# Score buffers, PV batches and lent banks in a fused attention and FFN block on one Trainium2 core

## The chip, the cores and the metric

The kernel runs on one core of a Trainium2 chip. The metric is the device time of one execution in microseconds (us). The median of the runs is quoted, and the profiles are of single executions, whose span is some 2 us shorter than the time of the same run.

## The reference, cut to what matters

One adaptive-layernorm transformer block: sequence S = 2048, width D = 1024, 32 query heads of 32 channels that share one key and one value head, FFN width 3584, bfloat16 data.

```python
h = layernorm(x) * (1 + ca) + sa            # sa, ca, ga, sb, cb, gb = silu(c) @ w_mod
q = h @ wq                                  # 32 heads of 32 channels
k, v = h @ wk, h @ wv                       # one head
p = softmax(q @ k.T * 32 ** -0.5)
x = x + ga * ((p @ v) @ wo)
h = layernorm(x) * (1 + cb) + sb
x = x + gb * ((silu(h @ w1) * (h @ w3)) @ w2)
```

## The kernel before

The kernel lists its operations as a graph, orders them on each engine with a list scheduler that uses guessed durations, and then emits a fixed order per engine. The program does not change this order at run time; a wrong guess in it is paid as a wait.

The queries are worked off in four blocks of 512. A block's attention has 8 head groups (4 heads each) of 16 key tiles. One **step** is one key tile for 4 heads: four score matmuls that run side by side in the array (four take 0.61 us together in the first timeline below), exponentials of 4 x 512 columns on ScalarE, and PV, which multiplies the exponentials with V. After a block's attention come its output projection, a layernorm and the FFN (called the post work). The post work of block b runs on TensorE in between the steps of block b+1. Hence nothing can fill TensorE in block 0, and the last block's post work stands alone at the end.

The kernel divides PSUM, the memory that TensorE writes its results to, into eight banks of 512 float32 columns. Before the change, five hold scores, one accumulates PV over 16 key tiles, and two (PB) serve everything else:

```python
S5 = nc.alloc_psum_tensor("S5", [P, 5, 512], F32)
A = nc.alloc_psum_tensor("A", [P, 512], F32)
PB = [nc.alloc_psum_tensor("PB%d" % i, [P, 512], F32) for i in range(2)]
# ... in attention, step i; u = i % 6 is the exponential buffer
s1 = 3 + i % 2
# four matmuls into banks 0, 1, 2 and s1                      writes "S3" and ("S1", s1)
e.activation(U[:, u, 0:3, :], S5[:, 0:3, :], ACT.Exp, scale=SCALE)    # 1536 columns, reads "S3"
e.activation(U[:, u, 3, :], S5[:, s1, :], ACT.Exp, scale=SCALE)       # 512 columns, reads ("S1", s1)
# ... after every second step: PV of two key tiles into A; VectorE sums U for the denominators
```

The three-bank part "S3" exists once. The scores of step i+1 can start only when the 1536-column exponential of step i has ended, and until they arrive ScalarE has just the 512-column exponential of step i to do. Call the ScalarE work that is left in that time the **cover**.

The softmax here doesn't subtract the row's maximum and nothing guards it: scores larger than these inputs give would overflow.

## Time and profile before

| | before |
|---|---|
| median of 4 runs (range) | 1398.92 us (1396.92 to 1401.57) |
| span of the profiled run | 1396.4 us |
| step 16 / 128 / 511 of 512 starts | 92.0 / 337.4 / 1196.7 us |
| last exponential ends | 1198.7 us |
| left after it (post work of block 3) | 197.7 us |

The first lines of the page give the busy time of each engine, then the busy share in tenths in 40 slices of the span, and the clock granted to TensorE in tenths of full speed. PE is TensorE, ACT is ScalarE, DVE is VectorE.

```profile
PE 1209.6 (87%) x8689; PEld 424.9 (30%) x8689; DVE 939.8 (67%) x1174; ACT 1046.8 (75%) x1142; POOL 17.3 (1%) x34
...
PE   4498985555899999988899999978999999789997
...
ACT  2378998888889999888899998989999989311100
...
PEclk9597995555899999998999999979999999889999
```

From about the third slice to the 34th, ScalarE is nearly always busy; the last six slices have almost no ScalarE work. TensorE is half idle, at half clock, in slices 7 to 10, which are the rest of block 0.

Groups of instructions; after the bar stand busy time and mean duration in ns, after the second bar the idle time just before them and what ended it. L613 and L615 are the two exponentials, L606 the scores.

```profile
L613 ACT ACTIVATE UREG<-S 128x1536 bf16<-128x1536 f32 x512 | 744.1, 1453 | 150.7 <-PE S L606 140.1
...
L606 PE MATMUL S<-QT,KT 32*128 32x512 bf16 x2048 | 222.5, 425 | 121.5 <-ACT UREG L613 118.3
L615 ACT ACTIVATE UREG<-S 128x512 bf16<-128x512 f32 x512 | 305.7, 597 | 0.0
```

ScalarE waits 140.1 us for scores, always before the large exponential, never before the small one. The timeline shows how, in a stretch of block 0 where TensorE has nothing else to do (start and duration in us, engine, line, operation):

```profile
286.01 1.45 ACT L613 ACTIVATE UREG<-S 128x1536 bf16<-128x1536 f32 x1 [0.23 <-PE S L606]
287.36 0.59 ACT L615 ACTIVATE UREG<-S 128x512 bf16<-128x512 f32 x1
287.51 0.11 PEld L606 LDWEIGHTS S<-QT,KT 32*128 32x128 bf16 x4 [2.06 <-ACT UREG L613]
287.52 0.61 PE L606 MATMUL S<-QT,KT 32*128 32x512 bf16 x4 [1.56 <-ACT UREG L613]
...
288.18 1.45 ACT L613 ACTIVATE UREG<-S 128x1536 bf16<-128x1536 f32 x1 [0.23 <-PE S L606]
```

The large exponential ends at 286.01 + 1.45 = 287.46, its successor starts at 288.18: a **round trip** of 0.72 us through TensorE. The small exponential covers all but 0.23 us of it. A step takes 288.18 - 286.01 = 2.17 us. Nearly all steps between 205 and 330 us are like this one; three of them, at the ends of head groups, take 3.64 us, as 16 matmuls for the denominators (1.90 us) stand before the scores, so that the mean there is 2.25 us. Without the wait a step would take 1.83 us: consecutive starts are 1.35 us apart after a large exponential, and about 0.48 us after a small one.

With post work in the mix, TensorE is full as well, and the scores also stand behind FFN matmuls (L711) that the fixed order put first:

```profile
460.58 1.68 PE L711 MATMUL PB<-QT,WREG 128*128 128x512 bf16 x7
...
461.63 0.63 ACT L615 ACTIVATE UREG<-S 128x512 bf16<-128x512 f32 x1
462.20 0.10 PEld L606 LDWEIGHTS S<-QT,KT 32*128 32x128 bf16 x4 [0.42 <-ACT UREG L613]
...
462.65 1.45 ACT L613 ACTIVATE UREG<-S 128x1536 bf16<-128x1536 f32 x1 [0.39 <-PE S L606]
```

Busy time by stretch: length, then busy us (and instructions) of each engine, granted clock, DMA share, GB/s. The first stretch is block 0 with query projections to do, the second the rest of block 0, the third block 1 with post work, the last the post work of block 3.

```profile
91.50:205.00 113.50, 104.78 (x929) 37.21 (x928) 91.20 (x108) 103.16 (x107) 0.00 (x0) 0.91 0.21 66
205.00:330.00 125.00, 65.94 (x496) 11.22 (x492) 68.70 (x66) 107.92 (x111) 0.00 (x0) 0.51 0.12 28
400.00:600.00 200.00, 198.16 (x1428) 67.85 (x1427) 148.16 (x172) 182.78 (x205) 0.00 (x0) 1.00 0.38 97
1200.00:1300.00 100.00, 88.18 (x409) 39.57 (x410) 46.72 (x75) 10.76 (x18) 1.47 (x3) 0.89 0.31 90
```

At the end, each of the eight groups of W2 (28 matmuls, L722) waits for the eviction of the previous one and its transpose (L732), so groups follow each other every 7.28 us although 28 matmuls need 6.06, at 0.216 us from start to start:

```profile
1339.91 6.21 PE L722 MATMUL PB<-HREG,WREG 128*128 128x512 bf16 x28
1346.96 0.40 PE L732 MATMUL PB<-IDENT,HREG 128*128 128x128 bf16 x4 [0.85 <-DVE HREG L725]
1347.19 6.21 PE L722 MATMUL PB<-HREG,WREG 128*128 128x512 bf16 x28
```

### The profile page before, as it was taken

To read this page: it belongs to the slowest core of one execution; us is meant where nothing else is said; L and a number is where in the kernel's file an instruction comes from. 1 tells how busy PE (TensorE), PEld (TensorE's weight loads), DVE (VectorE), ACT (ScalarE), POOL (GpSimd) and SP (SyncE) were. 2 spreads that over 40 slices of the span, in tenths; PEclk is the share of its full clock that TensorE was granted. 3 is DMA by queue.
4 is the path that set the end of the run, shared out by engine and by line. 5 is a ranking of instruction groups with operands and counts; after the bars stand their busy time and mean duration, and the time that the engine had idled before them with its cause. 6 is when DMAs were issued, how large, how long until landed. Compare 5 with 4: busy or idle time off the path is not lost.

```text
span 1396.4 us, 21161 instructions
## 1 busy us (share of the span) xinstructions
PE 1209.6 (87%) x8689; PEld 424.9 (30%) x8689; DVE 939.8 (67%) x1174; ACT 1046.8 (75%) x1142; POOL 17.3 (1%) x34
## 2 busy tenths in 40 slices
PE   4498985555899999988899999978999999789997
PEld 3233320000233333322333333322333333234443
DVE  5777775555777777668877876678777766644421
ACT  2378998888889999888899998989999989311100
POOL 1000000000000000000000000000000000000000
PEclk9597995555899999998999999979999999889999
DMA  8306013000024334450133334421333345225544
GB/s 319 122 31 197 1 34 80 1 1 0 1 61 120 93 97 102 85 116 25 46 106 91 107 102 80 87 80 31 91 106 107 91 88 98 57 63 154 146 79 110
DMA packets 252928, 118.93 MB, mean 85 GB/s; under 512 B 120736, under 2 KB 244640, under 8 KB 252832
## 3 DMA queue, kind: packets, MB, share of 16 engines
q1 hardware_dynamic: 252832, 117.59, 31.6%
q8 instruction: 68, 1.11, 0.3%
q14 instruction: 28, 0.23, 0.1%
HBM read 113.38 MB, written 4.19 MB: 84 GB/s over the span
## 4 chain that ended last, share of the span: by engine, by line
PE 77%; ACT 11%; DVE 7%; issue 3%; POOL 1%; DMA 0%; SPq 0%; DVEq 0%; POOLq 0%; ACTq 0%
PE PB L703 15%; PE PB L711 15%; PE PB L722 14%; PE S L606 13%; ACT UREG L613 9%; PE A L624 7%; PE PB L682 4%; PE PB L506 4%; PE PB L658 3%; DVE ST L421 2%; DVE UREG L646 2%; ACT UREG L615 1%; DVE XN L438 1%; PE PB L452 1%; PE PB L490 1%
## 5 line engine op out<-in xcount | busy, mean ns | idle before, releaser
L613 ACT ACTIVATE UREG<-S 128x1536 bf16<-128x1536 f32 x512 | 744.1, 1453 | 150.7 <-PE S L606 140.1
L646 DVE TENSOR_TENSOR UREG<-UREG 128x2048 bf16<-128x2048 bf16 x256 | 310.9, 1214 | 82.8 <-ACT UREG L615 82.4
L606 PE MATMUL S<-QT,KT 32*128 32x512 bf16 x2048 | 222.5, 425 | 121.5 <-ACT UREG L613 118.3
L615 ACT ACTIVATE UREG<-S 128x512 bf16<-128x512 f32 x512 | 305.7, 597 | 0.0
L703 PE MATMUL PB<-QT,WREG 128*128 128x512 bf16 x896 | 226.6, 386 | 1.3 <-DVE QT L467 1.3
L640 DVE TENSOR_TENSOR UREG<-UREG 128x2048 bf16<-128x2048 bf16 x128 | 155.6, 1215 | 106.3 <-ACT UREG L615 105.7
L711 PE MATMUL PB<-QT,WREG 128*128 128x512 bf16 x896 | 222.6, 381 | 0.0
L722 PE MATMUL PB<-HREG,WREG 128*128 128x512 bf16 x896 | 214.3, 380 | 0.0
L624 PE MATMUL A<-UREG,V 128*32 128x512 bf16 x2048 | 178.3, 429 | 6.5 <-ACT UREG L615 5.6
L606 PEld LDWEIGHTS S<-QT,KT 32*128 32x128 bf16 x2048 | 52.2, 92 | 350.9 <-ACT UREG L613 320.7
L706 ACT ACTIVATE HREG<-PB 128x512 bf16<-128x512 f32 x112 | 67.0, 599 | 116.3 <-PE PB L703 116.3
L708 DVE SCALAR_TENSOR_TENSOR HREG<-HREG,PB 128x512 bf16<-128x512 bf16 x112 | 76.0, 679 | 88.9 <-ACT HREG L706 88.9
L667 DVE RECIPROCAL DSB<-DSB 128x128 f32<-128x128 f32 x128 | 116.7, 932 | 0.9
L703 PEld LDWEIGHTS PB<-QT,WREG 128*128 128x128 bf16 x896 | 80.1, 98 | 118.8 <-issue 43.0
L711 PEld LDWEIGHTS PB<-QT,WREG 128*128 128x128 bf16 x896 | 81.0, 98 | 111.9 <-issue 29.0
L722 PEld LDWEIGHTS PB<-HREG,WREG 128*128 128x128 bf16 x896 | 79.2, 98 | 108.0 <-issue 30.3
L714 DVE TENSOR_TENSOR HREG<-HREG,PB 128x512 bf16<-128x512 bf16 x112 | 76.7, 685 | 20.3 <-PE PB L711 18.8
L682 PE MATMUL PB<-WO,QT 128*128 128x512 bf16 x256 | 67.9, 414 | 4.9 <-DVE QT L669 4.9
L506 PE MATMUL PB<-HREG,WREG 128*128 128x512 bf16 x256 | 63.9, 385 | 0.1
L725 DVE TENSOR_SCALAR HREG<-PB,MODC 128x512 bf16<-128x512 f32 x32 | 24.0, 749 | 53.6 <-PE PB L722 53.6
L624 PEld LDWEIGHTS A<-UREG,V 128*32 128x32 bf16 x2048 | 31.8, 96 | 85.1 <-issue 38.6
L452 PE MATMUL PB<-IDENT,XN 128*128 128x128 bf16 x256 | 28.1, 263 | 26.8 <-DVE XN L438 17.5
(56 smaller groups left out, 436.1 us busy)
## 6 DMA issues: line engine op xcount, KB each, us to landing
WREG<-in_B_w_dram SPq DMA_DIRECT2D x112, 512.0 KB, 3.7
WREG<-in_B_w_dram SPq DMA_DIRECT2D x32, 896.0 KB, 5.8
X<-in_A_x_dram SPq DMA_DIRECT2D x8, 1024.0 KB, 5.7
WREG<-in_w_mod_dram SPq DMA_DIRECT2D x16, 512.0 KB, 4.6
UREG<-in_w_mod_dram SPq DMA_DIRECT2D x8, 512.0 KB, 8.7
out_dram<-X SPq DMA_DIRECT2D x4, 1024.0 KB, 6.3
WO<-in_A_wo_dram SPq DMA_DIRECT2D x1, 2048.0 KB, 15.5
WREG<-in_A_wq_dram SPq DMA_DIRECT2D x1, 1792.0 KB, 10.7
```

The costliest lines, as they stand in the source:

```text
L506: g = mm_group(NC, lambda e, b, c: e.matmul(b[:], WQ[:, c, f * P:(f + 1) * P], HT[:, c, sl], start=c == 0, stop=c == NC - 1), lambda c: [( ...
L606: r = e.matmul(S5[:, b, j * qn:(j + 1) * qn], KT[32 * gg:32 * gg + 32, kt * P:(kt + 1) * P], QT[32 * gg:32 * gg + 32, f, q0:q0 + qn], star ...
L613: G.add("act", lambda e, u=u: e.activation(U[:, u, 0:3, :], S5[:, 0:3, :], ACT.Exp, scale=SCALE), reads=["S3"], writes=[("U", u, 0)] + uk, ...
L615: G.add("act", lambda e, u=u, s1=s1: e.activation(U[:, u, 3, :], S5[:, s1, :], ACT.Exp, scale=SCALE), reads=[("S1", s1)], writes=[("U", u, ...
L624: r = e.matmul(A[32 * gg:32 * gg + 32, 0:qn], V[:, kt, :], U[:, pu, gg, j * qn:(j + 1) * qn], start=kt == 0, stop=kt == NT - 1, tile_posit ...
L640: G.add("dve", lambda e, tr=tr, u=u, fu=first_u: e.tensor_tensor(TR[:, tr, :], U[:, fu].rearrange("p g s -> p (g s)"), U[:, u].rearrange(" ...
L646: G.add("dve", lambda e, tr=tr, u=u: e.tensor_tensor(TR[:, tr, :], TR[:, tr, :], U[:, u].rearrange("p g s -> p (g s)"), ALU.add), reads=[( ...
L667: G.add("dve", lambda e, h=h: e.reciprocal(DSB[:, h * 128:(h + 1) * 128], DSB[:, h * 128:(h + 1) * 128]), reads=["DSB"], writes=[("DSBr", ...
L682: g = mm_group(NC, lambda e, b, f, t=t, h=h: e.matmul(b[:], QT[:, f, t * P:(t + 1) * P], WO[:, f, h * 512:(h + 1) * 512], start=f == 0, st ...
L703: g1 = mm_group(NC, lambda e, b, c, sl=sl, sub=sub: e.matmul(b[:, 0:qn], W1S[:, sl, c, sub * P:(sub + 1) * P], QT[:, c, q0:q0 + qn], start ...
L711: g3 = mm_group(NC, lambda e, b, c, sl=sl, sub=sub: e.matmul(b[:, 0:qn], W3S[:, sl, c, sub * P:(sub + 1) * P], QT[:, c, q0:q0 + qn], start ...
L722: g = mm_group(NF, lambda e, b, fc, sl=sl: e.matmul(b[:, 0:qn], W2S[:, sl, fc, :], HHT[:, fc, 0:qn], start=fc == 0, stop=fc == NF - 1), la ...
```

## The change

Its intent: three score buffers of two banks each, used in rotation, so that two exponentials of 1024 columns replace those of 1536 and 512, and the second one (twice as long as the small one before) covers the round trip. That takes six banks, so PV loses its bank: it goes through the two shared banks in batches of eight key tiles, each batch then added to an SBUF accumulator by VectorE. Ten exponential buffers instead of six hold a batch. Before the first scores and after the last, the six score banks are lent to other work. Some smaller things come along: separate orders of bank use for projection, FFN and W2 transposes, x and the output moved per tile of 128 rows, another place for two small tensors (to make room), and support for blocks of 256 queries, which is not used.

```diff
-    S5 = nc.alloc_psum_tensor("S5", [P, 5, 512], F32)
-    A = nc.alloc_psum_tensor("A", [P, 512], F32)
-    PB = [nc.alloc_psum_tensor("PB%d" % i, [P, 512], F32) for i in range(2)]
+    SP = nc.alloc_psum_tensor("SP", [P, 3, 2, 512], F32)
+    PB = [nc.alloc_psum_tensor("PB%d" % i, [P, 512], F32)[:] for i in range(2)]
+    PB += [SP[:, b, h, :] for b in range(3) for h in range(2)]
-    NU = 6
+    NU = 10
+    VB = 8
 # ... in attention, step i
-                s1 = 3 + i % 2
+                bufs = [(2 * i) % 3, (2 * i + 1) % 3]
 # ... four score matmuls into the four banks of bufs[0] and bufs[1]
-                # (exponentials of S5[:, 0:3, :] and S5[:, s1, :])
+                for h in range(2):
+                    G.add("act", lambda e, u=u, h=h, b=bufs[h]: e.activation(
+                        U[:, u, 2 * h:2 * h + 2, 0:npk * qn], SP[:, b, :, 0:npk * qn], ACT.Exp, scale=SCALE), ...)
-                if len(pend) == 2:
-                    # PV of two key tiles, accumulated in A over all 16
+                if len(pend) == vb:
+                    # PV of eight key tiles in four parts of two, in one shared bank g; the first part
+                    # waits for all eight tiles:
+                        dep = pend if w0 == 0 else pend[w0:w0 + 2]
+                    # then ASB = bank (first batch of a head group) or ASB += bank, on VectorE
 # ... in the scheduler, the order of PV against other work
-                    elif n.cls == "V":
-                        backlog = sum(1 for x in ready["pe"] if x.cls == "V")
-                        r = 1 if (att or backlog >= 3) else 4
-                    elif n.cls == "D":
-                        r = 2
+                    elif n.cls is not None:
+                        r = 1 if att or t - n.est > 1.0 else 4
 # ... in free_banks(): score banks are "closed" from the first scores to the last exponential
+                if b in closed:
+                    continue
-    span = G.schedule([0, 1])
+    span = G.schedule(range(8))
```

## The prediction

> **What bounds it now.** Per-stretch table, stretches of 25 us: a sparse prologue to about 84 us; attention of block 0 to about 365; blocks 1 to 3, each overlapped with the previous block's output projection and FFN, to 1198; then the last block's FFN alone, 198 us, TensorE-bound. Inside attention ScalarE is the pacing engine: about 92% busy (22.9 of 25 us) with FFN work, 21.3 of 25 without. Groups by line: 512 exponentials of 1536 columns (1453 ns) and 512 of 512 (597 ns), with 150.7 us idle before them, 140 of it released by the score matmuls. Timeline: starts are 1.35 and about 0.48 us apart when back to back, so a step needs 1.83 us of ScalarE. It takes 2.17 us in block 0 (about 283 us) and about 2.3 with FFN work (tanh included).
>
> The cause: the three-bank score buffer is single. Next scores start when the 1536-column exponential ends and arrive 0.72 us later at half TensorE clock (about 0.5 at full), while only the 512-column one (0.48 us) covers that. With FFN work, score matmuls also stand behind about seven or eight FFN matmuls (0.216 us each); TensorE reads 100% busy there.
>
> **What the change does.** Exponential columns and instruction count per step stay the same: two of 1024, an estimate of 0.92 us apart each from the two sizes above, so 1.83 us again. But the score round trip (0.5 to 0.72 us) now hides behind 0.92 us. I expect the 0.23 us stall in quiet stretches to vanish, except around PV batches.
>
> TensorE: PV every second step costs 0.54 us for 0.43 us of streaming, plus about 0.1 us; batches of eight save an estimated 5 to 8 us per block. Against that, PV shares two banks with the FFN (short stalls), and each head group gets one more VectorE add (0.7 us, hidden: VectorE is 67% busy).
>
> Binding resource afterwards: per block ScalarE needs 128 x 1.83 + 28 x 0.49 = 248 us; TensorE about 260 (736 matmuls x 0.216 = 159, scores 55, PV 33, rest 14). So blocks 1 to 3 become TensorE-bound. The Trainium skill ("TensorE: Matmul & The Clock Gate", the HAM clock gate) says the array runs at half clock unless kept busy; the trace agrees: granted clock 0.50 to 0.58 between 200 and 350 us. There a packed PV batch takes 0.52 us a tile and may delay scores.
>
> Sum, in us: prologue -6 (VectorE-bound, so little); block 0 steps 2.17 to about 1.95: -27; blocks 1 to 3, 2.20 to about 2.05: -55; tail -10 (the timeline shows about 1.1 us lost at each of eight W2 groups, waiting for eviction and transpose before the next group); part of block 2's FFN spills behind attention: +4.
>
> **Predicted: 1305 us, 80% range 1270 to 1345.** Chances: faster by over 2% 0.90, within 2% 0.07, slower 0.03.
>
> **What would show it.** ScalarE idle before exponentials released by scores falls from 140 to below 60 us; 1024-column exponentials near 1.02 us busy, 0.92 apart; quiet stretches of block 0 at 1.85 to 1.95 us a step; last exponential at about 1110; tail about 188 us with W2 groups back to back; TensorE 95% busy through blocks 1 to 3.
>
> **What would make it wrong.** The static order was computed for guessed durations: if it packs FFN matmuls or PV parts before scores, ScalarE still waits (time above 1345). If PV holding a bank starves the FFN of its two banks, TensorE gaps appear and much of an FFN spills past attention. If TensorE has more slack than I count, the time is below 1270.

## The result, and the profile after

The median went from 1398.92 to 1312.04 us (four runs each; 1310.45 to 1313.19 after). A ratio in this text is the mean time of one kernel's fast runs over that of the other's of the same rounds, so it is not quite the ratio of the medians. Here it is 0.9377, 95% interval 0.9358 to 0.9396: 6.2% faster.

| us | before | after | difference |
|---|---|---|---|
| step 16 starts | 92.0 | 91.3 | -0.7 |
| step 128 starts (block 1 begins) | 337.4 | 320.6 | -16.8 |
| step 511 starts | 1196.7 | 1105.8 | -90.9 |
| last exponential ends | 1198.7 | 1107.7 | -91.0 |
| work left after it | 197.7 | 200.9 | +3.2 |
| span | 1396.4 | 1308.6 | -87.8 |

The page of the profile after:

```profile
PE 1138.8 (87%) x8561; PEld 439.4 (34%) x8689; DVE 958.9 (73%) x1206; ACT 1015.3 (78%) x1142; POOL 17.1 (1%) x35
...
PE   5387896455779999999899999999999999999998
...
ACT  1368988999999999999979999998999998011100
...
PEclk8688996666889999999999999999999999999999
```

The busy share of TensorE's matmuls is 87% before and after, though 88 us are gone. This is what the Trainium skill ("Perfetto Trace Analysis", Identifying the Most-Contended Engine) warns of: it calls matmul busy time a bad measure of distance to the roofline (the best that the hardware allows), and advises the share of weight loads, among others, in its place. The traces agree: PEld rose from 30% to 34%. The page after also has 8561 matmul records for 8689 weight loads, so that its PE time is a little too low, and matmuls are counted by their weight loads below where it matters.

The groups after; L656 has both exponentials of a step.

```profile
L656 ACT ACTIVATE UREG<-SP 128x1024 bf16<-128x1024 f32 x1024 | 968.5, 1067 | 85.5 <-PE SP L646 65.9
...
L646 PE MATMUL SP<-QT,KT 32*128 32x512 bf16 x2048 | 215.4, 411 | 100.0 <-ACT UREG L656 93.9
```

The wait for scores fell from 140.1 to 65.9 us, of which the list of waits shows 24.6 us as one single wait in the prologue (21.0 before). Without it, the wait fell from 119.1 to 41.3 us. The quiet part of block 0, first between PV batches and then at one:

```profile
260.82 12.94 ACT L656 ACTIVATE UREG<-SP 128x1024 bf16<-128x1024 f32 x14 [0.28 <-PE SP L646]
...
267.40 0.61 PE L646 MATMUL SP<-QT,KT 32*128 32x512 bf16 x4 [1.22 <-ACT UREG L656]
...
269.23 0.61 PE L646 MATMUL SP<-QT,KT 32*128 32x512 bf16 x4 [1.22 <-ACT UREG L656]
...
272.07 1.90 PE L670 MATMUL PB<-UREG,V 128*32 128x512 bf16 x16 [0.39 <-ACT UREG L656]
...
274.57 11.17 ACT L656 ACTIVATE UREG<-SP 128x1024 bf16<-128x1024 f32 x12 [0.81 <-PE SP L646]
```

Fourteen exponentials run with no gap, and scores follow each other every 269.23 - 267.40 = 1.83 us. Then two parts of a PV batch (L670, 16 matmuls) take 1.90 us at half clock; the scores behind them are late, and ScalarE stands for 0.81 us. With these waits, a step of this stretch takes 125 / 62 = 2.02 us on average (124 exponentials in the second line below). The same stretches as before, at the same places of the span:

```profile
91.50:205.00 113.50, 99.75 (x925) 37.75 (x935) 91.82 (x110) 103.06 (x111) 0.00 (x0) 0.94 0.20 61
205.00:330.00 125.00, 64.97 (x564) 15.86 (x564) 78.79 (x80) 113.99 (x124) 0.00 (x0) 0.63 0.14 32
400.00:600.00 200.00, 193.71 (x1473) 71.18 (x1497) 164.22 (x188) 197.01 (x225) 0.00 (x0) 1.00 0.36 92
1200.00:1300.00 100.00, 99.47 (x476) 46.02 (x485) 29.68 (x46) 8.96 (x15) 0.00 (x0) 1.00 0.52 121
```

Between 400 and 600 us ScalarE is now 98.5% busy (197.01 of 200; 182.78 before), with TensorE busy for 193.71 us (1473 matmul records for 1497 weight loads, so some are missing).

TensorE read full in this stretch before the change too, and yet the kernel gained 74 us in blocks 1 to 3. Besides the work that was pushed behind the last exponential (below), the traces show two things; no run separates them. First, around the change from one block to the next, the old post work is over and the new has hardly begun: from 600 to 675 us TensorE was busy for 59.39 of 75 us before, and its clock fell at times. From step 128 to the last exponential the clock was at half for 66 us before and for 23 us after, while TensorE's idle time there is about the same (52.9 and 51.4 us). Second, it changes less often between kinds of matmuls (scores, PV, denominators, full-size ones): 952 times in that part before and 793 after, by the order of the weight loads. Between 400 and 600 us, at full clock, the median from start to start is 0.31 us at a change and 0.216 between full-size matmuls, so that 159 changes fewer are an estimated 16 us.

The tail lost its gaps; a W2 group (28 matmuls of L794, here over two lines because of the bank name) and its transposes (L811) take 1272.04 - 1265.77 = 6.27 us:

```profile
1265.77 0.39 PE L811 MATMUL SP<-IDENT,HREG 128*128 128x128 bf16 x4
1265.99 4.91 PE L794 MATMUL SP<-HREG,WREG 128*128 128x512 bf16 x22
1270.74 1.46 PE L794 MATMUL PB<-HREG,WREG 128*128 128x512 bf16 x6
1272.04 0.39 PE L811 MATMUL SP<-IDENT,HREG 128*128 128x128 bf16 x4
```

Yet the work left after the last exponential did not get shorter. After it the trace counts 353 weight loads for W2, and block 3 has only 224: 129 matmuls of block 2, about 129 x 0.216 = 27.9 us, had not been done in time.

### The profile page after: what moved, and what is told of

Its sections match the earlier page's. It is cut to its first block, busy times and chain, and to the rows that moved or that the text cites. A ratio compares the mean times of both kernels' runs of the same rounds, so it can differ in the third digit from the quotient of the medians.

```text
span 1308.6 us, 21172 instructions
## 1 busy us (share of the span) xinstructions
PE 1138.8 (87%) x8561; PEld 439.4 (34%) x8689; DVE 958.9 (73%) x1206; ACT 1015.3 (78%) x1142; POOL 17.1 (1%) x35
## 4 chain that ended last, share of the span: by engine, by line
PE 58%; ACT 25%; DVE 9%; issue 6%; DMA 1%; POOL 1%; SPq 0%; DVEq 0%; ACTq 0%
ACT UREG L656 24%; PE PB L765 13%; PE PB L794 10%; PE PB L670 8%; PE SP L646 7%; PE SP L765 6%; PE SP L794 4%; PE PB L546 3%; PE PB L738 2%; ACT HREG L774 2%; DVE UREG L697 2%; DVE ST L461 1%; DVE UREG L702 1%; PE PB L712 1%; PE SP L738 1%
## 5 line engine op out<-in xcount | busy, mean ns | idle before, releaser
L656 ACT ACTIVATE UREG<-SP 128x1024 bf16<-128x1024 f32 x1024 | 968.5, 1067 | 85.5 <-PE SP L646 65.9
L765 PE MATMUL PB<-QT,WREG 128*128 128x512 bf16 x1397 | 343.3, 381 | 9.1 <-issue 6.4
L646 PE MATMUL SP<-QT,KT 32*128 32x512 bf16 x2048 | 215.4, 411 | 100.0 <-ACT UREG L656 93.9
L765 PEld LDWEIGHTS PB<-QT,WREG 128*128 128x128 bf16 x1456 | 125.7, 98 | 176.2 <-issue 52.3
L646 PEld LDWEIGHTS SP<-QT,KT 32*128 32x128 bf16 x2048 | 52.0, 92 | 313.4 <-ACT UREG L656 287.0
L794 PE MATMUL PB<-HREG,WREG 128*128 128x512 bf16 x612 | 153.3, 380 | 4.0 <-issue 2.5
L670 PE MATMUL PB<-UREG,V 128*32 128x512 bf16 x2016 | 142.9, 419 | 6.2 <-ACT UREG L656 5.8
L794 PEld LDWEIGHTS PB<-HREG,WREG 128*128 128x128 bf16 x644 | 55.3, 98 | 73.5 <-issue 22.9
L765 PE MATMUL SP<-QT,WREG 128*128 128x512 bf16 x330 | 74.5, 379 | 0.3
L670 PEld LDWEIGHTS PB<-UREG,V 128*32 128x32 bf16 x2016 | 48.0, 101 | 78.9 <-issue 32.4
L546 PE MATMUL PB<-HREG,WREG 128*128 128x512 bf16 x243 | 62.2, 389 | 1.7 <-DVE QT L549 0.8
L794 PE MATMUL SP<-HREG,WREG 128*128 128x512 bf16 x245 | 56.0, 379 | 0.4
L765 PEld LDWEIGHTS SP<-QT,WREG 128*128 128x128 bf16 x336 | 32.8, 98 | 39.4
```

The costliest lines, as they stand in the source:

```text
L546: g = mm_group(NC, lambda e, b, c: e.matmul(b, WQ[:, c, f * P:(f + 1) * P], HT[:, c, sl], start=c == 0, stop=c == NC - 1), lambda c: [("WQ ...
L646: r = e.matmul(SP[:, bufs[gg // 2], gg % 2, j * qn:(j + 1) * qn], KT[32 * gg:32 * gg + 32, kt * P:(kt + 1) * P], QT[32 * gg:32 * gg + 32, ...
L656: G.add("act", lambda e, u=u, h=h, b=bufs[h]: e.activation(U[:, u, 2 * h:2 * h + 2, 0:npk * qn], SP[:, b, :, 0:npk * qn], ACT.Exp, scale=S ...
L670: r = e.matmul(PB[g.bank][32 * gg:32 * gg + 32, 0:qn], V[:, kt, :], U[:, pu, gg, j * qn:(j + 1) * qn], start=w0 + n == 0 and j == 0, stop= ...
L765: return e.matmul(b[:, o:o + qn], w13[w][:, sl, c, sub * P:(sub + 1) * P], QT[:, c, q0:q0 + qn], start=c == 0, stop=c == NC - 1)
L794: return e.matmul(b[:, j * qn:(j + 1) * qn], W2S[:, (d0 + j) % 2, fc, :], HHT[:, fc, 0:qn], start=fc == 0, stop=fc == NF - 1)
```

## The experiments

My theory, from the prediction: the change gains because more ScalarE work covers the round trip of the scores; from the first FFN on TensorE has no slack, so what costs TensorE time costs the whole. Rivals: PV batches and lent banks relieve TensorE and that is the gain; or ScalarE, 98% busy in the blocks, is the only bound left. All times are medians of four runs; each call shared its runs of the kernel before (1399.3 to 1399.6 us), and ratios are to those. The comparison with the reference passed for all, also for the two that are wrong: their error is below what it sees.

### e1_old_scores: the old score buffers in the new kernel

```diff
-                bufs = [(2 * i) % 3, (2 * i + 1) % 3]
+                s1 = 3 + i % 2
 # scores into banks 0, 1, 2 and s1; exponentials of 1536 and 512 columns as before; bank 5 unused
```

> The changed kernel with the old score buffers put back (three single banks and one bank of two, exponentials of 1536 and 512 columns); PV batches of eight, lending and the scheduler stay. Theory (the gain is the longer cover of the score round trip): most of the gain goes, 1370 us (1350 to 1395), ScalarE idle before the large exponential back above 110 us in all, quiet steps of block 0 at 2.1 us or more. Rival (the gain is TensorE relief by PV batches and lent banks): 1312 to 1330 us.

Measured: 1388.44 us, ratio 0.992 (0.9906 to 0.9935). ScalarE's wait for scores is back at 126.2 us:

```profile
L656 ACT ACTIVATE UREG<-SP 128x1536 bf16<-128x1536 f32 x512 | 744.0, 1453 | 141.5 <-PE SP L647 126.2
```

A step of the quiet stretch takes 2.25 us on average (55 large and 56 small exponentials between 205 and 330 us), as in the kernel before (56 and 55). All the rest of the change together is worth 11 us without the buffers. The theory's number was slightly too low; the rival is out.

### e2_pv2: PV in batches of two

```diff
-    VB = 8
+    VB = 2
```

> The changed kernel with PV in batches of two key tiles through the shared banks instead of eight. Theory (TensorE has no slack after block 0, so every regrouping counts): 48 more PV batches per block at 0.1 to 0.2 us each plus bank contention, 1335 us (1322 to 1360), the time appearing as more FFN left after the last exponential. Rival (batch size is only tidiness, scores set the pace): 1305 to 1318 us. VectorE gets 12 additional adds of 0.7 us per head group of 512 queries less 4, some 130 us in all, which may show as waits of its own.

Measured: 1407.96 us, ratio 1.0055 (1.0039 to 1.0072): 0.6% slower than the kernel before. The direction was the theory's, the size (96 us instead of 23) was not. ScalarE keeps its pace, and the last exponential ends at 1095.5 us, even earlier than in the kernel after; but 310 us of work are left behind it. Between 400 and 1090 us, with as many scores done, the FFN got this far in the kernel after (first fence; L765 are W1 and W3) and in this run (second fence):

```profile
L765 PE MATMUL PB<-QT,WREG 128*128 128x512 bf16 x1245 | 306.7, 381 | 8.1 <-issue 6.2 <-DVE QT L507 0.3 <-DVE HREG L776 0.2
L646 PE MATMUL SP<-QT,KT 32*128 32x512 bf16 x1344 | 132.7, 385 | 14.7 <-ACT UREG L656 13.3
```

```profile
L765 PE MATMUL PB<-QT,WREG 128*128 128x512 bf16 x872 | 227.1, 391 | 8.2 <-DVE ASB L685 5.5 <-DVE QT L507 1.1 <-DVE HREG L781 0.7
L646 PE MATMUL SP<-QT,KT 32*128 32x512 bf16 x1344 | 134.3, 390 | 36.8 <-ACT UREG L656 36.3
...
L670 PE MATMUL PB<-UREG,V 128*32 128x512 bf16 x1344 | 102.0, 386 | 35.0 <-DVE ASB L685 23.5 <-DVE ASB L682 4.2 <-DVE HREG L800 2.3
```

W1 and W3 did 872 matmuls instead of 1297 (by their weight loads; 1245 have a record), and PV waits for L685, the adds that empty the shared banks. The cost comes after block 0: step 128 starts at 308.1 us, 12.5 us earlier than in the kernel after. (The expectation's count of adds is garbled: batches of two need eight per head group of 512 queries instead of two, 192 further ones in all.)

### e3_no_lend: score banks never lent

```diff
-                if b in closed:
+                if b in closed or b >= 2:
```

> The changed kernel with the six score banks never lent: other work has the two shared banks throughout. Theory: only both ends change; the start loses 0 to 4 us, the tail gets back the waits between W2 groups (about 1 us each in eight groups) and slower projections: 1324 us (1316 to 1332). Rival (lending does nothing, the separate chain for the W2 transposes already frees the tail): 1310 to 1315 us.

Measured: 1317.27 us, ratio 0.941 (0.9396 to 0.9424), so lending is worth about 5 us, just at the edge of what the intervals separate. Its last exponential ends 2 us later and the rest takes 5 us more. One reason that I gave was wrong: the W2 groups in its tail also follow every 6.27 us. So that gain does not come from lent banks. The transposes' own order of bank use is the likely source; no run takes it out alone.

### e4_before_pv9: batches of eight in the kernel before

```diff
-    NU = 6
+    NU = 9
-                if len(pend) == 2:
+                for w0 in range(0, len(pend), 2) if len(pend) == 8 else ():
 # four parts of two tiles into A, as in the change; the first waits for all eight
```

> The kernel before with PV in batches of eight alone (own PV bank kept, nine exponential buffers instead of six, as many as fit). Theory (the score round trip paces the kernel before): little, 1388 us (1375 to 1400), ScalarE idle before the large exponential still above 120 us. Rival (PV batches are the main gain): 1330 to 1360 us.

Measured: 1412.59 us, ratio 1.0087 (1.007 to 1.0104), 0.9% slower. ScalarE's wait for scores stays at 124.2 us. Batches alone gain nothing here. The run is not quite the change's batching: only nine exponential buffers fit beside the rest, so one is spare instead of two, and ScalarE waits 32.5 us for PV in the whole run (6.8 between 400 and 600 us), more than the 13 us that the run loses. TensorE did get its relief: from step 128 to the last exponential it changes 791 times between kinds of matmuls instead of 952, but a kernel that waits for scores and buffers cannot use it.

### e5_two_bufs: no cover at all

```diff
-                bufs = [(2 * i) % 3, (2 * i + 1) % 3]
+                bufs = [0, 1]
-                if b in closed:
+                if b in closed or b >= 6:
```

> The changed kernel with only two of its three score buffers used and no rotation, so that the next scores wait for both exponentials and nothing covers their round trip (the third buffer's banks stay out of use). Theory (what counts is how much ScalarE work covers the round trip: 0 here, 0.48 us before, 0.92 us after): a quiet step of block 0 costs 1.83 + 0.1 + 0.7 = 2.6 us at half TensorE clock, 2.4 at full; in all 1312 + 128 x 0.7 + 384 x 0.5 less the slack of TensorE, 1530 us (1450 to 1600). Rival (the buffers matter only through fewer bank conflicts and the order of work): under 1400 us.

Measured: 1659.76 us, ratio 1.1856 (1.1839 to 1.1874). The quiet steps are as computed:

```profile
301.84 1.94 ACT L656 ACTIVATE UREG<-SP 128x1024 bf16<-128x1024 f32 x2 [0.72 <-PE SP L646]
303.83 0.11 PEld L646 LDWEIGHTS SP<-QT,KT 32*128 32x128 bf16 x4 [2.55 <-ACT UREG L656]
...
304.50 1.94 ACT L656 ACTIVATE UREG<-SP 128x1024 bf16<-128x1024 f32 x2 [0.72 <-PE SP L646]
```

The wait is the whole round trip, 0.72 us, and the step 2.66 us. This gives one rule for three kernels: a quiet step takes the longer of 1.83 us and the time until the freeing exponential ends plus 0.72 us. That is 1.94 + 0.72 = 2.66 here, 1.45 + 0.72 = 2.17 before, and 1.02 + 0.72 = 1.74, hence 1.83, after. In all I had expected less (1450 to 1600 us): I credited the blocks with TensorE slack, but 145 exponentials between 400 and 600 us mean 2.76 us a step there, tanh included.

### e6_exp_narrow: less ScalarE work (wrong result)

```diff
-                        U[:, u, 2 * h:2 * h + 2, 0:npk * qn], SP[:, b, :, 0:npk * qn], ACT.Exp, scale=SCALE),
+                        U[:, u, 2 * h:2 * h + 2, 0:448], SP[:, b, :, 0:448], ACT.Exp, scale=SCALE),
 # the scheduler is told; exponential buffers 8 and 9 are set once, the others hold loaded weights
```

> Wrong result on purpose: each exponential of the changed kernel does 896 of its 1024 columns, 0.107 us less for each of 1024, 109 us of ScalarE work in all; the scheduler is told. Theory (TensorE has no slack once the first FFN starts, so only block 0 gains): 1287 us (1275 to 1300), the last exponential 60 us or more earlier but the FFN work left after it longer by nearly as much. Rival (the kernel after is bound by ScalarE through the attention blocks): 1205 to 1235 us.

Measured: 1295.73 us, ratio 0.9259 (0.9243 to 0.9274). ScalarE's busy time fell by 98 us (1015.3 to 917.1), the whole by 16, and about 12 of those come before step 128, which starts at 309.1 us instead of 320.6. So ScalarE at 98% busy was not what bounded the blocks. TensorE is what is left, as the theory says: it reads 192.57 of 200 us busy between 400 and 600 us, and ScalarE now waits there for it (no run takes work from TensorE alone):

```profile
400.00:600.00 200.00, 192.57 (x1451) 71.38 (x1476) 161.69 (x189) 177.06 (x221) 0.00 (x0) 1.00 0.37 93
...
L657 ACT ACTIVATE UREG<-SP 128x896 bf16<-128x896 f32 x1024 | 861.9, 928 | 155.6 <-PE PB L671 86.7
```

One detail was different: the last exponential came about 27 us earlier, not 60, since ScalarE waits 86.7 us in all for PV to free exponential buffers, and less FFN work was pushed behind.

### e7_pv_half: one PV part at a time in the quiet stretch

```diff
-                              dur=len(pend[w0:w0 + 2]) * (npk * qn / 2400 + 0.007), ...
+                              dur=len(pend[w0:w0 + 2]) * (0.7 if q0 == 0 and f >= 3 else npk * qn / 2400 + 0.007), ...
```

> The changed kernel, the scheduler told that a pair of PV tiles takes 1.4 us in heads 3 to 7 of block 0, so that it puts one pair and not two between scores while the array is at half clock. Theory (two pairs, 1.9 us at half clock, hold the scores up there): ScalarE idle between 205 and 330 us falls from 11.0 to under 4 us and the whole by about as much, as block 0 is in front of everything: 1304 us (1298 to 1309). Rival (spread PV delays denominators or frees buffers late): 1310 or more.

Measured: 1306.73 us, ratio 0.9339 (0.9323 to 0.9356). ScalarE's idle time between 205 and 330 us fell from 11.0 to 5.8 us, less than expected: only 1.2 us of it is for scores, 4.6 us is a new wait for exponential buffers that the spread PV frees later.

### e8_ends256: shorter blocks at both ends

```diff
-    BLOCKS = [(i * 512, 512) for i in range(NTB)]
+    BLOCKS = [(0, 256), (256, 512), (768, 512), (1280, 512), (1792, 256)]
```

> The changed kernel with blocks of 256, 512, 512, 512, 256 queries instead of four of 512 (the code has the case; it reads the FFN weights five times instead of four). Theory (TensorE is idle in much of block 0 and full from the first FFN to the end, so starting the FFN some 120 us earlier moves the end): 1245 us (1220 to 1285). Rival (ScalarE bound, or the extra pass of weights makes the short blocks DMA bound): 1300 us or more.

Measured: 1371.85 us, ratio 0.9798 (0.9784 to 0.9813), 60 us slower than the kernel after: my theory's forecast failed. Three stretches of this run:

```profile
400.00:450.00 50.00, 25.26 (x208) 6.06 (x208) 29.70 (x29) 45.68 (x51) 0.00 (x0) 0.60 0.00 0
...
1250.00:1300.00 50.00, 38.74 (x320) 32.36 (x320) 16.16 (x39) 7.69 (x20) 0.00 (x0) 0.93 0.75 197
1300.00:1350.00 50.00, 32.43 (x240) 25.68 (x240) 6.92 (x18) 1.54 (x4) 0.00 (x0) 0.80 0.56 109
```

First, the idle time only moved: the post work of 256 queries is done by 400 us, while the attention of 512 queries goes on, and TensorE is half idle again. Second, 265.2 us of work are left after the last exponential instead of 200.9, 64 us more, and this holds the whole loss. The attention of the last 256 queries is half as long as that of a block of 512, and much of the post work of the block before did not fit beside it: 327 matmuls of 512 columns of W1 and W3 and 219 of W2 come after the last exponential, about 546 x 0.216 = 118 us, though the last block's own FFN has matmuls of 256 columns only. Third, the fifth pass over the FFN weights runs beside half as much arithmetic: in the tail the DMA share is 0.56 to 0.75, TensorE is idle for 47 of the 265 us (7 of 201 in the kernel after), and weight loads by DMA take 4% of the chain of work that ended last. No run separates the second from the third. The theory is not refuted by this, but it was not enough: it counted TensorE's idle time and not what the shorter block adds.

### e9_pv4: PV in batches of four

```diff
-    VB = 8
+    VB = 4
```

> The changed kernel with PV in batches of four. If each further batch costs the same (96 us for 192 further batches in the run with batches of two, 0.5 us each), 64 further batches give 1344 us (1334 to 1356). If the two shared banks only starve beyond some rate, it stays near 1312 to 1322.

Measured: 1342.6 us, ratio 0.9598 (0.9582 to 0.9614). The cost of a further batch is the same from eight to four as on average from eight to two: about 0.5 us, with no threshold.

### e10_pv2_narrow: cheap evictions of batches of two (wrong result)

```diff
-    VB = 8
+    VB = 2
-                        G.add("dve", lambda e, g=g: e.tensor_tensor(ASB[:, 0:qn], ASB[:, 0:qn], PB[g.bank][:, 0:qn],
+                        G.add("dve", lambda e, g=g: e.tensor_tensor(ASB[:, 0:64], ASB[:, 0:64], PB[g.bank][:, 0:64],
```

> Wrong result on purpose: batches of two as in the run before, but the seven adds that take each later batch out of its bank do 64 of 512 columns, so VectorE has about 0.47 us less per batch and 100 us less in all, while TensorE's grouping is the same. If the cost of small batches is their eviction, which holds one of two shared banks and VectorE: back to 1345 us (1320 to 1370). If it is TensorE's regrouping between PV and other matmuls: 1385 us or more.

Measured: 1343.8 us, ratio 0.9607 (0.9592 to 0.9621). Of the 96 us that batches of two cost, 64 are the length of the evictions; 32 are left for more frequent hand-overs, regrouping and what the short adds still cost. The regrouping is some 10 of these by an estimate: 896 changes between kinds of matmuls instead of 793 from step 128 to the last exponential, at 0.1 us. The run doesn't tell VectorE's time from the time for which a bank is held, as both shrink together.

### e11_fixed_map: no rotation

```diff
-                bufs = [(2 * i) % 3, (2 * i + 1) % 3]
+                bufs = [0, 1 + i % 2]
```

> The changed kernel without the rotation: the first score buffer is always buffer 0, the second alternates between 1 and 2. The cover of the round trip is the same 0.92 us. Theory (the cover counts, not the rotation): 1312 us (1307 to 1317). Rival (rotation matters): more than 1320.

Measured: 1310.82 us, ratio 0.9371 (0.9353 to 0.9389), the same as the kernel after. The rotation is not needed. One single buffer and one double buffer of two banks give the same cover.

### e12_pv_early: a try at a better kernel

```diff
-                        dep = pend if w0 == 0 else pend[w0:w0 + 2]
+                        dep = pend if w0 == 0 and not (q0 == 0 and f >= 3) else pend[w0:w0 + 2]
 # and the durations of e7
```

> A try at a better kernel: in heads 3 to 7 of block 0, where nothing else needs the banks, each PV pair waits for its own two tiles only and is spread as in the run with 1.4 us a pair. In that run ScalarE idle between 205 and 330 us was 5.8 us, 4.6 of it for exponential buffers not yet free. Theory (that was left of it): under 3 us idle and 1302 us (1297 to 1306). Rival (no more to win there): 1306 to 1312.

Measured: 1302.48 us (1301.7 to 1304.36), ratio 0.9311 (0.9297 to 0.9325), against 0.9377 (0.9358 to 0.9396) for the kernel after. It beats both kernels, and in its own call it is 8 us under the run without rotation, which equals the kernel after. ScalarE's idle time in the quiet stretch fell less than expected, in the group of exponentials between 205 and 330 us from 11.0 us in the kernel after to 4.5 us here:

```profile
L656 ACT ACTIVATE UREG<-SP 128x1024 bf16<-128x1024 f32 x132 | 122.1, 1065 | 4.5 <-PE SP L646 2.2 <-PE PB L670 2.2
```

## Why the prediction was right or wrong, point by point

The prediction was 1305 us with a range from 1270 to 1345; measured were 1312.04. Its mechanism held, and some terms of its sum were off by 10 to 20 us in both directions. That the total is so near, and that the last exponential ends at 1107.7 us where about 1110 was forecast, is in part luck: block 0 gained 16 us less than forecast and blocks 1 to 3 gained 19 us more.

- **"So blocks 1 to 3 become TensorE-bound"**: right as far as the runs go, though ScalarE reads 98.5% busy there. Taking 98 us from ScalarE gave 16 us (e6), 12 of them in front of block 1. The forecast that TensorE is 95% busy in these blocks reads 93.5% (735.7 of 787.1 us, with some records missing).
- **"The score round trip now hides behind 0.92 us", the quiet stall vanishes "except around PV batches"**: right. Steps take 1.83 us between batches, and the rule from e5 gives all three kernels. The undo run (e1) returns 76 of the 87 us.
- **"Blocks 1 to 3, 2.20 to about 2.05: -55"**: the step after is 2.05 us ((1105.8 - 320.6) / 383), as predicted. The step before was 2.24 ((1196.7 - 337.4) / 383), not 2.20, so that the term is -74. The prediction let block 0 end at about 365 us where step 128 starts at 337.4, and so gave blocks 1 to 3 too little time. This was the largest error in the sum, and in favour of the change.
- **"Block 0 steps 2.17 to about 1.95: -27", "prologue -6"**: mis-sized. Step 16 starts only 0.7 us earlier. From step 16 to 128 it went from 245.4 to 229.3 us, 16 us, or 2.19 to 2.05 us a step. In the first half (91.5 to 205 us) TensorE is busy with query projections before and after (92% and 88% of the time), and the quiet half takes 2.02 us a step, not the 1.85 to 1.95 that were to show it: it still has the PV waits that e7 and e12 then partly removed.
- **"Tail -10", "spills behind attention: +4"**: measured +3 in place of -6. The spill was 27.9 us, not 4; the last block's own work got shorter by the difference, about 25 us, as gaps closed (the W2 groups alone 8 x 1 us) and, as it seems, spilled work filled the layernorm gap: TensorE is idle for 7 us after the last exponential, 24 before.
- **"Batches of eight save an estimated 5 to 8 us per block"**: the size fits for TensorE's own time (159 changes fewer, an estimated 16 us in three blocks), but the use of the batches was missed. In the kernel before the saving is worth nothing by itself (e4, which however lacks a tenth exponential buffer). What counts is that the wide buffers take PV's own bank: with PV in shared banks, batches of two cost 96 us (e2), and batches of eight keep that cost away. The buffers with small batches (1408 us) do not beat the kernel before (1399 us), the rest of the change without the buffers gains 11 us (e1, 1388 us), and all together give 1312.
- **Extra VectorE adds "hidden"**: right for batches of eight, wrong as a general statement. In e2 they hold banks, and 64 of its 96 us go with their length (e10).
- **"ScalarE idle ... below 60 us", "1024-column exponentials near 1.02 us busy, 0.92 apart"**: 65.9 us, a near miss; the spacing was right, 12.94 us for 14 of them, but their mean busy time reads 1.067 us. In e5, where every second one follows a pause, it is 1.021.

Not settled: how much of e2's cost is VectorE's time and how much the held banks, whether the batches would gain in the kernel before with a tenth exponential buffer, and what the scheduler's new order is worth by itself, as no run takes it out alone.

## What to carry to other kernels

Measure the round trip of a buffer from the end of the work that frees it to the start of the work that needs it, and compare it with the work that its consumer has in between; split buffers so that this cover is longer than the round trip, and don't spend effort on rotation for its own sake. If the wider buffers take an accumulator away, count the evictions that replace it: the parts of such a change can be worth little or lose alone and win together. An engine that reads 98% busy need not be the bound; take work off it and see.

## What the Trainium skill lacked or had wrong

- "TensorE: Matmul & The Clock Gate" (Why this matters for your kernels) says that one should leave no TensorE gap above about 3 us to stay at full clock. In the kernel before, no wait for an exponential ahead of score matmuls is longer than 1.6 us (2.1 us ahead of their weight loads), and the granted clock of the quiet stretch (205 to 330 us) is still 0.51. The page has such short pauses between groups of matmuls as a second way to lose the clock (A second HAM failure mode), but no threshold for such thin and regular work.
- "ScalarE: Activation LUTs" (What ACT_TABLE_LOAD costs) gives 186 ns + 0.833 ns per column for immediates, and an overlap of about 93 ns. That fits 1453 and 597 ns at 1536 and 512 columns (an estimate of 1466 and 613 by the formula), which overlap by 0.10 and 0.12 us here. It doesn't have that exponentials of 1024 columns read 1067 ns on average instead of the 1021 of e5, with starts 0.91 us apart back to back ((12.94 - 1.07) / 13), an overlap of about 0.15 us.
- "PSUM — Partial Sum Buffer" has no cost for breaking an accumulation into parts that other engines must take out: here about 0.5 us for each further PV batch (31 us for 64 of them, 96 us for 192).
- No page that I used says how long scores take from one engine through TensorE and back: 0.72 us from the end of one exponential to the start of the next at half clock, for four 32-row matmuls of 512 columns.
